# Layernorm folded into the first Fourier product of a GFNet + GEGLU block

## The chip, the cores and the metric

The kernel runs on one core of a Trainium2 chip. The metric is the device time of one execution in microseconds (us). TensorE is called PE in the profile, VectorE DVE, ScalarE ACT, GpSimd POOL; SP is the engine that issues most DMAs. PEld is TensorE's weight load.

## The reference

Two residual blocks are applied to x of 2048 rows by 576 columns, in bfloat16:

```python
def _layernorm(x, axis=-1, eps=1e-5):
    m = jnp.mean(x, axis=axis, keepdims=True)
    v = jnp.var(x, axis=axis, keepdims=True)
    return (x - m) / jnp.sqrt(v + eps)
...
    X = jnp.fft.rfft2(x.astype(jnp.float32), axes=(-2, -1))   # block A
    X = X * (w_r + 1j * w_i)
    y = jnp.fft.irfft2(X, s=(2048, 576), axes=(-2, -1)).astype(jnp.bfloat16)
...
    return (_gelu(x @ w_gate) * (x @ w_up)) @ w_down           # block B, 576 -> 4608 -> 576
...
    h = x + A(_layernorm(x));  h2 = h + B(_layernorm(h))
```

## The kernel before

The kernel has three parts. The **head** loads x, takes the layernorm statistics of its 16 tiles and does the first step of the row Fourier transform. The **spectral part** does the column transform, the rest of the row transform, the product with the filter and the way back. The **feed-forward part** is the gate and up products (L941), GELU, and the down product (L984, L1003), with the second layernorm spread among them. The change touches the head alone.

`h_sb` holds x as [128 partitions, 16 tiles h, 576]: row 16p + h lies on partition p of tile h. Six DMAs on SP's queue bring it in, for tiles 0-1, 2-3, 4-5, 6-7, 8-11 and 12-15 (L75). The 2048-row transform is split as 128 x 16, and `row16(h)` (L300) does the part over the 128 partitions of one tile: it multiplies the tile with the table `F16`, a 128 x 128 matrix of scaled sines that `row_table` builds (its zeros stand for the coset that a row does not belong to). Columns d and d + 288 are folded on the way: the product of the first half of the columns with [F, F] and of the second half with [F, -F] are added in PSUM, so 256 output columns hold sum and difference. So `F16` has three planes, F, F and -F, and `minus_row` makes the last. For each tile that is four products of 128 x 128 weights (a piece of the tile) with 256 moving columns (L308). The 64 + 64 remaining columns of each tile are done by `row16_rest` (L321), four tiles after another into one PSUM tile `f4`: two products of 64 weight columns with 128 moving columns for a tile (L324), in two column groups of the array.

The operand of these products is `xn`, a normalised copy of the tile: `norms(lo, hi)` (L362) has DVE write (x - mean) * rstd for one tile (L137), then calls `row16`. The statistics come in two ways. For tiles 0, 2, 4, 6, 8, 10 and 12 to 15 DVE does it (`sd`, L352: two bn_stats and, one tile later or by `flush`, a bn_aggr). For tiles 1, 3, 5, 7, 9 and 11 ACT does it (`ln_act`, L121: two passes with an accumulator, each followed by a read of the accumulator), and `ln_fin` on POOL turns the sum of squares into a variance. `ln_rstd` (L131) makes rstd for four tiles at a time on POOL, an addition and a power.

ACT takes the products out of PSUM into `Bt`: `evict` (L332) for two tiles at a time, `evict4` (L339) for the rests of four, the last of these on DVE. PSUM tiles with the tag "two" come from one ring of four; a new one waits until the one four before it has been read. `fill` (L295) issues products whose result nobody reads: 16 ahead of tile 0, 6 in `small_table`, 3 ahead of tile 8.

`small_table` (L401) transposes F by PE for the table `G16` of the way back. `phases`, `drop_sign`, `col_sin` and `mirror` make the column table `DT`: DVE computes phases `pd` and their absolute values `kd`, ACT takes the sines, and `mirror(r)` writes the second half as a signed mirror image, r = 1 on ACT and r = 0 on DVE. `first_a`, `angle_*`, `sine`, `cosine` and `minus_sine` make the table `TF` of the other part of the row transform. `gather(0)` and `gather(1)` (L370) are indirect DMAs of POOL's queue for the mirrored rows of the filter; SP's queue moves them into `WR` and `WI` later (L471), POOL scales two columns of these (L479), and DVE first uses them at L586.

The order of each engine's instructions is that of the program (`tc.manual_schedule()`), so the lines L414 to L490, written out by hand, are the schedule of the head. The first product of the spectral part is `f2` (L518), on `Bt`, `DT` and `DF`.

Of the kernel before, what the change touches and what calls it, by code (L numbers as in the profile page):

```python
# [42 lines left out]
def kernel_body(  # L43
# [44 lines left out]
    V.memset(mhalf[:], -0.5)  # L88

# [11 lines left out]
    F16 = keep.tile([P, 3, P], BF16, name="F16")  # L101
# [29 lines left out]
    def ln_rstd(dst, src, lo, hi):  # L131
        sl = slice(lo, hi)
        G.tensor_scalar(dst[:, sl], src[:, sl, 1], 1e-5, None, op0=ALU.add)  # L133
        G.tensor_tensor(dst[:, sl], dst[:, sl], mhalf[:, sl], ALU.pow)  # L134

# [137 lines left out]
    def phases():  # L273
        for t in range(3):
            V.scalar_tensor_tensor(
                pd[:, t, :], iJ[:], iD[:, t : t + 1], kd[:, t, :], op0=ALU.mult, op1=ALU.add
            )

    def row_table():
        V.scalar_tensor_tensor(  # L280
            F16[:, 0:2, :],
            iu[:].rearrange("p c l -> p (c l)").unsqueeze(1).to_broadcast([P, 2, P]),
            0.0,
            fs[:].unsqueeze(1).to_broadcast([P, 2, P]),
            op0=ALU.is_equal,
            op1=ALU.mult,
        )

    def minus_row():
        V.tensor_scalar(F16[:, 2, :], F16[:, 0, :], -1.0, None, op0=ALU.mult)  # L290

# [8 lines left out]
    def row16(h):  # L300
        if h % 2 == 0:
            ps_f[h] = two("f2t")
        f2t, b = (ps_f[h], 0) if h in ps_f else (ps_f[h - 1], 1)
        fill(f2t[:, b, :], FILL.get(h, 0))
        x = xn[:, h, :]
        for t in range(2):
            for n, d0 in ((0, t * P), (1, DH + t * P)):
                T.matmul(  # L308
                    f2t[:, b, t * 2 * P : (t + 1) * 2 * P],
                    lhsT=x[:, d0 : d0 + P],  # L310
                    rhs=F16[:, n : n + 2, :],
                    start=(n == 0),
                    stop=(n == 1),
                )

# [5 lines left out]
    def row16_rest(h):  # L321
        o = (h % 4) * P
        for p0, d0 in ((0, 256), (64, 512)):
            T.matmul(  # L324
                ps_f["f4", h - h % 4][p0 : p0 + 64, 0, o : o + P],
                lhsT=xn[:, h, d0 : d0 + 64],
                rhs=F16[:, 0, :],
                start=True,
                stop=True,
            )  # L330
# [16 lines left out]
    def flush():  # L347
        while agg:
            h, st = agg.pop()
            V.bn_aggr(mv[:, h, :], st[:])  # L350
# [11 lines left out]
    def norms(lo, hi):  # L362
        for h in range(lo, hi):
            normalise(V, xn[:, h, :], mv, rstd, h)
            row16(h)
# [11 lines left out]
    xn_pool = tc.tile_pool(name="xn", bufs=1, side="right")  # L377
    xn = xn_pool.__enter__().tile([P, H, D], BF16, name="xn")
# [10 lines left out]
    def mirror(r):  # L389

        for a in range(2):
            dst, src, sg = DT[:, :, a, r, JM - a : JH - a], DT[:, :, a, r, JM - 2 :: -1], sgn[:, r : r + 1]
            if r:
                A.activation(dst, src, ACT.Copy, scale=sg)
            else:
                V.tensor_scalar(dst, src, sg, None, op0=ALU.mult)
# [18 lines left out]
    for h in (1, 3, 5, 7, 9, 11):  # L415
        ln_act(h)
# [3 lines left out]
    sd(0, 2)  # L420
    minus_row()
    sd(4)
    ln_fin(slice(1, 4, 2))
    ln_rstd(rstd, mv, 0, 4)
    phases()
    sd(6)
    flush()
    norms(0, 4)
    rests(0)
    drop_sign(kd[:], pd[:])  # L430
    ln_fin(slice(5, 8, 2))
    ln_rstd(rstd, mv, 4, 8)
    gather(0)
    evict(0, 2)
    evict4(0)
    sd(8)
    norms(4, 8)
    rests(4)
    small_table()
    gather(1)  # L440
    sd(10, 12)
    ln_fin(slice(9, 12, 2))
    ln_rstd(rstd, mv, 8, 12)
    first_a()
# [5 lines left out]
    mirror(1)  # L450
    sd(13, 14, 15)
    flush()
    norms(8, 12)
    ln_rstd(rstd, mv, 12, 16)
    rests(8)
# [6 lines left out]
    evict4(8)  # L462
    mirror(0)
# [28 lines left out]
    xn_pool.__exit__(None, None, None)  # L492
# [570 lines left out]
```

## Time and profile before

| | |
|---|---|
| time, median of 3 runs | 495.87 us (495.71 to 495.88) |
| the profiled execution: its time, its span | 495.85 us, 494.1 us |
| instructions | 12754 |
| busy: PE, PEld, DVE, ACT, POOL | 484.4, 339.1, 223.8, 160.1, 28.9 us |
| granted TensorE clock | full in every slice |
| HBM | 111 GB/s over the span |

The span is the time between the first and the last instruction of the program that the profiler saw; the execution's own time has 1.75 us more around it. A row of the timeline has a start in us from the start of the span, the time the group took, engine, line, operation, tiles written and read, shape and count, and in brackets the engine's idle time before it with what ended it. PE's records overlap: a product's record holds its way through the array as well, so the distance from one start to the next is what it costs a stream.

### The profile page before, as it was taken

How to read it: one execution, taken by the hardware profiler on the slowest of the kernel's cores; microseconds unless marked ns; L12 is line 12 of the kernel's file. 1: busy time of each engine (PE TensorE's matmuls, PEld its weight loads, DVE VectorE, ACT ScalarE, POOL GpSimd, SP SyncE). 2: the span in 40 equal slices, each digit the busy share in tenths (PEclk: the TensorE clock that was granted, in tenths of full speed). 3: DMA queues.
4: the chain of work that ended last, by engine and by line, in shares of the span. 5: the costliest groups of instructions: out<-in, count | busy, mean ns of one | idle time of the engine just before them, and what ended most of it. 6: DMA issues, size and time to landing. Idle time of an engine off the chain costs nothing.

```text
span 494.1 us, 12754 instructions
## 1 busy us (share of the span) xinstructions
PE 484.4 (98%) x5711; PEld 339.1 (69%) x5711; DVE 223.8 (45%) x448; ACT 160.1 (32%) x285; POOL 28.9 (6%) x79
## 2 busy tenths in 40 slices
PE   6899999999999999999999999999999999999997
PEld 3578789875589955555599855555799655555995
DVE  8999784798622167433311344333121333333111
ACT  8999873333210022233200133232110232232000
POOL 8500010011110001000000000000000000000000
PEclk9999999999999999999999999999999999999999
DMA  8748978959990039987730079977700287770000
GB/s 282 211 91 154 253 137 219 181 107 217 209 194 3 1 101 179 211 159 146 146 71 3 19 173 187 195 148 146 145 3 1 85 159 154 156 146 3 13 15 24
DMA packets 89549, 62.33 MB, mean 126 GB/s; under 512 B 23190, under 2 KB 88086, under 8 KB 89494
## 3 DMA queue, kind: packets, MB, share of 16 engines
q1 hardware_dynamic: 89206, 60.34, 60.6%
q0 software_dynamic: 288, 1.18, 0.8%
q8 instruction: 44, 0.72, 0.7%
q14 instruction: 11, 0.09, 0.1%
HBM read 52.65 MB, written 2.36 MB: 111 GB/s over the span
## 4 chain that ended last, share of the span: by engine, by line
PE 93%; DVE 0%; issue 0%
PE gu L941 57%; PE acc L984 27%; PE cs_ps L677 2%; PE acc L1003 2%; PE eo_ps L626 2%; PE pq_ps L518 1%; PE y_ps L813 1%; PE gh_ps L536 1%; PE gh_ps L535 1%; PE eo_ps L650 0%; PE pt L882 0%; DVE h_sb L1010 0%
## 5 line engine op out<-in xcount | busy, mean ns | idle before, releaser
L941 PE MATMUL gu<-Bt,wgu 64*128 64x512 bf16 (+1 forms) x2646 | 270.7, 363 | 0.0
L941 PEld LDWEIGHTS <-wgu 64*128 64x128 bf16 x2646 | 152.5, 94 | 114.6 <-issue 0.3
L950 DVE TENSOR_TENSOR P_sb<-g_sb,gu 128x512 bf16<-128x512 f32 (+1 forms) x156 | 100.4, 645 | 140.3 <-ACT g_sb L949 140.3
L949 ACT ACTIVATE g_sb<-gu 128x512 f32<-128x512 f32 (+1 forms) x156 | 88.0, 564 | 193.5 <-PE gu L941 193.5
L984 PEld LDWEIGHTS <-P_sb 64*128 64x128 bf16 x2160 | 123.1, 94 | 9.9
L984 PE MATMUL acc<-wd,P_sb 64*128 64x288 bf16 x1440 | 90.9, 283 | 0.0
L993 DVE TENSOR_TENSOR part<-part,acc 128x576 f32<-128x576 f32 x15 | 11.3, 755 | 112.6 <-ACT part L992 112.6
L992 ACT COPY part<-acc 128x576 f32<-128x576 f32 x15 | 9.6, 639 | 122.8 <-PE acc L984 122.8
L984 PE MATMUL acc<-wd_a,P_sb 64*128 64x288 bf16 x720 | 46.8, 283 | 0.0
L518 PE MATMUL pq_ps<-DT,Bt 128*128 128x290 bf16 x64 | 12.3, 286 | 0.8 <-ACT Bt L334 0.8
L941 PE MATMUL gu<-Bt,wgu_e 64*128 64x256 bf16 (+1 forms) x162 | 12.5, 305 | 0.0
L838 DVE TENSOR_SCALAR hrow<-h_sb,mv,rstd 128x1152 bf16<-128x1152 bf16 x14 | 12.2, 869 | 0.6 <-POOL rstd L876 0.6
L995 DVE TENSOR_TENSOR h_sb<-h_sb,part 128x576 bf16<-128x576 bf16 x15 | 11.4, 758 | 0.5
L518 PEld LDWEIGHTS <-Bt 128*128 128x128 bf16 x96 | 9.2, 97 | 3.3 <-ACT Bt L334 1.0
L134 POOL TENSOR_TENSOR rstd<-rstd,mhalf 128x1 f32<-128x1 f32 (+1 forms) x16 | 11.2, 699 | 1.3
L941 PEld LDWEIGHTS <-wgu_e 64*128 64x128 bf16 x162 | 10.3, 94 | 1.2
L133 POOL TENSOR_SCALAR rstd<-mv 128x1 f32<-128x1 f32 (+1 forms) x16 | 4.2, 265 | 116.2 <-DVE mv L119 115.9
L677 PE MATMUL cs_ps<-DQ,EO 58*128 58x290 bf16 x144 | 10.8, 283 | 0.0
L298 PE MATMUL f2t<-h_sb,ident 128*128 128x512 bf16 x19 | 6.4, 503 | 3.9 <-DMA h_sb<-in_A_x_dram 3.7
L529 ACT CAST pq<-pq_ps 128x580 bf16<-128x580 f32 x15 | 9.8, 665 | 0.4 <-PE pq_ps L518 0.2
L677 PEld LDWEIGHTS <-EO 58*128 58x128 bf16 x160 | 7.8, 94 | 2.4 <-issue 0.7
L308 PE MATMUL f2t<-F,xn 128*128 128x256 bf16 x64 | 7.7, 273 | 1.3 <-DVE xn L137 1.3
(145 smaller groups left out, 278.9 us busy)
## 6 DMA issues: line engine op xcount, KB each, us to landing
wgu<-in_B_w_gate_dram SPq DMA_DIRECT2D x46, 432.0 KB, 5.2
wgu<-in_B_w_up_dram SPq DMA_DIRECT2D x46, 432.0 KB, 6.9
wd_a<-in_B_w_down_dram SPq DMA_DIRECT2D x1, 1728.0 KB
wd<-in_B_w_down_dram SPq DMA_DIRECT2D x1, 1728.0 KB
wd<-in_B_w_down_dram SPq DMA_DIRECT2D x6, 288.0 KB, 10.5
out_dram<-h_sb SPq DMA_DIRECT2D x3, 576.0 KB, 2.8
h_sb<-in_A_x_dram SPq DMA_DIRECT2D x4, 288.0 KB, 4.0
h_sb<-in_A_x_dram SPq DMA_DIRECT2D x2, 576.0 KB
```

The costliest lines, as they stand in the source:

```text
L134: G.tensor_tensor(dst[:, sl], dst[:, sl], mhalf[:, sl], ALU.pow)
L518: T.matmul(ps[:, par, 0:JP], lhsT=Bt[:, t, col], rhs=DT[:, t // 2, par] if t < 4 else DF[:, par], start=(t == par), stop=(t == 4),)
L626: T.matmul(pv[:, n], lhsT=z[:, a, w].rearrange("p b j -> p (b j)"), rhs=TI[:, ts[k], 1 - a : 3 - a, :], start=(a == 0), stop=(a == 1),)
L677: T.matmul(ps[:, e, 0:JP], lhsT=EO[x][rows, w, 2 * g : 2 * g + 2].rearrange("p h e k l -> p (h e k l)"), rhs=DQ[rows, w] if w or e else DT ...
L838: V.tensor_scalar(hrow[:], h_sb[:, h, :].rearrange("p (r k) -> p r k", k=64).unsqueeze(2).to_broadcast([P, NR, 2, 64]), mv2[:, h, 0:1], rs ...
L941: T.matmul(gu[:, c, 0:n], lhsT=w[rows, r, i * P : (i + 1) * P], rhs=hl[tcnk % 2][rows, r, lo:hi], start=(r == 0), stop=(r == NR - 1),)
L949: A.activation(g_sb, gu[:, 0, 0:n], ACT.Gelu_apprx_tanh)
L950: V.tensor_tensor(p_sb(f)[:, lo:hi], g_sb, gu[:, 1, 0:n], ALU.mult)
L984: T.matmul(accs[i][:, c, 0:DH], lhsT=p_sb(f)[rows, st * P : (st + 1) * P], rhs=wd[f // NWA][rows, f % NWA, c * DH : (c + 1) * DH], start=( ...
L993: V.tensor_tensor(part, part, accs[1][:, :, 0:DH], ALU.add)
L995: V.tensor_tensor(hv, hv, part, ALU.add)
L1003: T.matmul(acc[:, 0, 0:DH], lhsT=p_sb(f)[:, st * P : (st + 1) * P], rhs=wd[f // NWA][:, f % NWA, cc], start=(f == 0), stop=(f == NFT - 1),)
```

## The change

The copy `xn` goes. `row16` and `row16_rest` take the tile `h_sb` itself as weights, and the moving operand is a table for each tile, `FR[:, h]` = rstd * [F, -F], made by DVE: 256 columns where the copy had 576. `F16` loses its doubled plane; the [F, F] operand is one plane of `FR` read twice by a stride of zero.

What the subtraction of the mean did is done by a further product in PSUM: the weights are -2 * mean (for the sum half) or -mean (for the rests) of the tile's rows, read 128 or 64 times by a stride of zero from `mneg`, and the moving operand is rstd * F, 128 columns. That is two more products for a tile in `row16` and two more in `row16_rest`, 64 in all. `mneg` is made by POOL, `minus_means`, one instruction after each `ln_rstd`, from a constant `neg` that DVE sets at the start.

Tile 7's statistics move from ACT to DVE. `mirror(1)` moves from ACT to DVE and stands behind the last tiles' tables. Some instructions stand elsewhere: two of the three phases, `drop_sign`, `evict(0, 2)`, both gathers, the statistics of tiles 14 and 15 and the tables of tiles 8 to 11.

```diff
--- before.py
+++ after.py
@@ -86,6 +86,10 @@
     nhpib = const("nhpib", -0.5 * PI)
     mhalf = keep.tile([P, H], FP32, name="mhalf")
     V.memset(mhalf[:], -0.5)
+    neg = keep.tile([P, 2], FP32, name="neg")
+    for i in range(2):
+        V.memset(neg[:, i : i + 1], -2.0 + i)
+    mneg = keep.tile([P, 2, H], BF16, name="mneg")
 
 
 
@@ -98,7 +102,7 @@
     ]
     ident = keep.tile([P, P], BF16, name="ident")
 
-    F16 = keep.tile([P, 3, P], BF16, name="F16")
+    F16 = keep.tile([P, 2, P], BF16, name="F16")
     G16 = keep.tile([P, 2, 2, P], BF16, name="G16")
 
 
@@ -132,6 +136,15 @@
         sl = slice(lo, hi)
         G.tensor_scalar(dst[:, sl], src[:, sl, 1], 1e-5, None, op0=ALU.add)
         G.tensor_tensor(dst[:, sl], dst[:, sl], mhalf[:, sl], ALU.pow)
+
+    def minus_means(lo, hi):
+        sh = [P, 2, hi - lo]
+        G.tensor_tensor(
+            mneg[:, :, lo:hi],
+            mv[:, lo:hi, 0].unsqueeze(1).to_broadcast(sh),
+            neg[:].unsqueeze(2).to_broadcast(sh),
+            ALU.mult,
+        )
 
     def normalise(eng, dst, m, r, h):
         eng.tensor_scalar(
@@ -270,24 +283,24 @@
             TI[:, sl].rearrange("p k r q -> p (k r) q"), TF[:, sl].rearrange("p k r q -> p (k r q)"), transpose=True
         )
 
-    def phases():
-        for t in range(3):
+    def phases(*ts):
+        for t in ts:
             V.scalar_tensor_tensor(
                 pd[:, t, :], iJ[:], iD[:, t : t + 1], kd[:, t, :], op0=ALU.mult, op1=ALU.add
             )
 
     def row_table():
         V.scalar_tensor_tensor(
-            F16[:, 0:2, :],
-            iu[:].rearrange("p c l -> p (c l)").unsqueeze(1).to_broadcast([P, 2, P]),
+            F16[:, 0, :],
+            iu[:].rearrange("p c l -> p (c l)"),
             0.0,
-            fs[:].unsqueeze(1).to_broadcast([P, 2, P]),
+            fs[:],
             op0=ALU.is_equal,
             op1=ALU.mult,
         )
 
     def minus_row():
-        V.tensor_scalar(F16[:, 2, :], F16[:, 0, :], -1.0, None, op0=ALU.mult)
+        V.tensor_scalar(F16[:, 1, :], F16[:, 0, :], -1.0, None, op0=ALU.mult)
 
     ps_f = {}
     FILL = {0: 16, 8: 3}
@@ -302,16 +315,24 @@
             ps_f[h] = two("f2t")
         f2t, b = (ps_f[h], 0) if h in ps_f else (ps_f[h - 1], 1)
         fill(f2t[:, b, :], FILL.get(h, 0))
-        x = xn[:, h, :]
+        x = h_sb[:, h, :]
+        plus = FR[:, h, 0:1, :].to_broadcast([P, 2, P])
         for t in range(2):
             for n, d0 in ((0, t * P), (1, DH + t * P)):
                 T.matmul(
                     f2t[:, b, t * 2 * P : (t + 1) * 2 * P],
                     lhsT=x[:, d0 : d0 + P],
-                    rhs=F16[:, n : n + 2, :],
+                    rhs=FR[:, h] if n else plus,
                     start=(n == 0),
-                    stop=(n == 1),
+                    stop=False,
                 )
+            T.matmul(
+                f2t[:, b, t * 2 * P : t * 2 * P + P],
+                lhsT=mneg[:, 0, h : h + 1].to_broadcast([P, P]),
+                rhs=FR[:, h, 0, :],
+                start=False,
+                stop=True,
+            )
 
     def rests(h):
         ps_f["f4", h] = two("f4")
@@ -320,14 +341,15 @@
 
     def row16_rest(h):
         o = (h % 4) * P
-        for p0, d0 in ((0, 256), (64, 512)):
-            T.matmul(
-                ps_f["f4", h - h % 4][p0 : p0 + 64, 0, o : o + P],
-                lhsT=xn[:, h, d0 : d0 + 64],
-                rhs=F16[:, 0, :],
-                start=True,
-                stop=True,
-            )
+        for mean in (False, True):
+            for p0, d0 in ((0, 256), (64, 512)):
+                T.matmul(
+                    ps_f["f4", h - h % 4][p0 : p0 + 64, 0, o : o + P],
+                    lhsT=mneg[:, 1, h : h + 1].to_broadcast([P, 64]) if mean else h_sb[:, h, d0 : d0 + 64],
+                    rhs=FR[:, h, 0, :],
+                    start=not mean,
+                    stop=mean,
+                )
 
     def evict(*hs):
         for h in hs:
@@ -361,7 +383,7 @@
 
     def norms(lo, hi):
         for h in range(lo, hi):
-            normalise(V, xn[:, h, :], mv, rstd, h)
+            V.tensor_scalar(FR[:, h], F16[:], rstd[:, h : h + 1], None, op0=ALU.mult)
             row16(h)
 
     wm = [tmp(n, [P, 8 * J], BF16) for n in ("wm_r", "wm_i")]
@@ -374,8 +396,8 @@
             in_offset=bass.IndirectOffsetOnAxis(ap=rev[:, 0:1], axis=0),
         )
 
-    xn_pool = tc.tile_pool(name="xn", bufs=1, side="right")
-    xn = xn_pool.__enter__().tile([P, H, D], BF16, name="xn")
+    fr_pool = tc.tile_pool(name="FR", bufs=1, side="right")
+    FR = fr_pool.__enter__().tile([P, H, 2, P], BF16, name="FR")
 
     def col_sin(r, src, bias):
         A.activation(
@@ -390,10 +412,7 @@
 
         for a in range(2):
             dst, src, sg = DT[:, :, a, r, JM - a : JH - a], DT[:, :, a, r, JM - 2 :: -1], sgn[:, r : r + 1]
-            if r:
-                A.activation(dst, src, ACT.Copy, scale=sg)
-            else:
-                V.tensor_scalar(dst, src, sg, None, op0=ALU.mult)
+            V.tensor_scalar(dst, src, sg, None, op0=ALU.mult)
 
     G16v = [G16[:, sign].rearrange("p x q -> p (x q)") for sign in range(2)]
     pt = []
@@ -412,47 +431,52 @@
                 )
 
     first, rest = slice(0, 2), slice(2, 9)
-    for h in (1, 3, 5, 7, 9, 11):
+    for h in (1, 3, 5, 9, 11):
         ln_act(h)
     G.memset(DF[:], 0.0)
     G.memset(DT[:, :, 1, :, JH - 1], 0.0)
     row_table()
-    sd(0, 2)
+    sd(0)
     minus_row()
-    sd(4)
+    sd(2, 4)
     ln_fin(slice(1, 4, 2))
     ln_rstd(rstd, mv, 0, 4)
-    phases()
-    sd(6)
+    minus_means(0, 4)
+    phases(0)
+    sd(6, 7)
     flush()
+    ln_fin(slice(5, 6))
+    ln_rstd(rstd, mv, 4, 8)
+    minus_means(4, 8)
+    gather(0)
     norms(0, 4)
     rests(0)
-    drop_sign(kd[:], pd[:])
-    ln_fin(slice(5, 8, 2))
-    ln_rstd(rstd, mv, 4, 8)
-    gather(0)
-    evict(0, 2)
-    evict4(0)
     sd(8)
     norms(4, 8)
     rests(4)
+    phases(1, 2)
     small_table()
-    gather(1)
+    evict(0, 2)
+    evict4(0)
     sd(10, 12)
+    drop_sign(kd[:], pd[:])
     ln_fin(slice(9, 12, 2))
     ln_rstd(rstd, mv, 8, 12)
+    minus_means(8, 12)
+    gather(1)
     first_a()
     col_sin(1, pd, zerob)
     col_sin(0, kd, hpib)
     evict(4, 6)
     evict4(4)
     A.activation(G16v[0], pt[0][:, 0, 0 : 2 * P], ACT.Copy, scale=G_SCALE)
-    mirror(1)
-    sd(13, 14, 15)
+    sd(13)
+    norms(8, 12)
+    rests(8)
+    sd(14, 15)
     flush()
-    norms(8, 12)
     ln_rstd(rstd, mv, 12, 16)
-    rests(8)
+    minus_means(12, 16)
     angle_b(first)
     angle_s(first)
     angle_c(first)
@@ -460,6 +484,7 @@
     rests(12)
     evict(8, 10)
     evict4(8)
+    mirror(1)
     mirror(0)
     V.tensor_copy(DF[0:32], D3[0:32])
     V.tensor_copy(DF[96:128], D3[96:128])
@@ -489,7 +514,7 @@
 
     load_dq(1)
 
-    xn_pool.__exit__(None, None, None)
+    fr_pool.__exit__(None, None, None)
     spw = tc.tile_pool(name="spw", bufs=1)
     wk = spw.__enter__()
     m1, m2 = (wk.tile([P, 2, 2, JP], BF16, name=n) for n in ("m1", "m2"))
```

## The prediction

> **What bounds the kernel now.** I read the page's chain first, then the chain of waits in order of time for the first 75 us, then the timeline of each engine through the head.
>
> ```profile
> span 494.1 us, 12754 instructions
> 31.09 0.04 issue
> 31.13 0.28 PE gh_ps L536
> ```
>
> The last two lines are the first pieces of the chain in order of time: from 31.13 us on it is TensorE without a break, to the end. So what the head does to the time is what it does to PE's start at 31.13, one for one. Next, PE's timeline up to there.
>
> ```profile
> 3.66 5.58 PE L298 MATMUL f2t<-h_sb,ident 128*128 128x512 bf16 x16 [3.66 <-DMA h_sb<-in_A_x_dram]
> 9.07 1.91 PE L308 MATMUL f2t<-F,xn 128*128 128x256 bf16 x16
> 10.91 0.41 PE L324 MATMUL f<-F,xn 128*64 128x128 bf16 x8
> 11.90 1.92 PE L308 MATMUL f2t<-F,xn 128*128 128x256 bf16 x16 [0.58 <-DVE xn L137]
> 13.76 0.41 PE L324 MATMUL f<-F,xn 128*64 128x128 bf16 x8
> 14.10 1.47 PE L298 MATMUL pt<-h_sb,ident 128*128 128x512 bf16 x6
> 15.50 0.30 PE L406 MATMUL pt<-ident,F 128*64 128x128 bf16 x4
> 16.08 0.81 PE L298 MATMUL f2t<-h_sb,ident 128*128 128x512 bf16 x3 [0.28 <-ACT Bt L334]
> 17.43 1.92 PE L308 MATMUL f2t<-F,xn 128*128 128x256 bf16 x16 [0.54 <-DVE xn L137]
> 19.28 0.41 PE L324 MATMUL f<-F,xn 128*64 128x128 bf16 x8
> 19.91 1.92 PE L308 MATMUL f2t<-F,xn 128*128 128x256 bf16 x16 [0.21 <-DVE xn L137]
> 22.97 0.67 PE L518 MATMUL pq_ps<-DT,Bt 128*128 128x290 bf16 x4 [0.80 <-ACT Bt L334]
> 30.60 0.30 PE L535 MATMUL gh_ps<-pq,TF 128*128 128x289 bf16 x1 [0.27 <-ACT TF L263]
> 31.13 0.28 PE L536 MATMUL gh_ps<-pq,TF 128*128 128x289 bf16 x1 [0.23 <-ACT pq L529]
> ```
>
> The four L308 rows are the four groups of tiles, each with its rests (L324). PE waits ahead of groups two, three and four: it is not the bound of the head. Who is, ACT's and DVE's rows show:
>
> ```profile
> 10.98 0.67 ACT L124 ACTIVATE junk<-h_sb 128x576 bf16<-128x576 bf16 x1
> 11.64 1.90 ACT L334 CAST Bt<-f2t 128x1024 bf16<-128x1024 f32 x2
> 17.58 0.85 ACT L394 ACTIVATE DT<-DT,sgn 128x216 bf16<-128x216 bf16 x2
> 20.99 1.93 ACT L334 CAST Bt<-f2t 128x1024 bf16<-128x1024 f32 x2
> 24.95 1.04 ACT L260 ACTIVATE TF<-pr,pib 128x896 bf16<-128x896 int32 x1 [0.38 <-DVE pr L251]
> 7.29 0.45 DVE L357 BATCH_NORM_STATS2 st<-h_sb 128x6 f32<-128x288 bf16 x1
> 8.20 0.21 DVE L350 BATCH_NORM_AGGREGATE mv<-st 128x2 f32<-128x12 f32 x1
> 8.42 1.45 DVE L137 TENSOR_SCALAR xn<-h_sb,mv,rstd 128x576 bf16<-128x576 bf16 x4
> 22.21 0.69 DVE L340 CAST Bt<-f 128x512 bf16<-128x512 f32 x1 [0.16 <-PE f L324]
> 24.00 0.26 DVE L266 TENSOR_SCALAR TF<-TF 128x256 bf16<-128x256 bf16 x1
> ```
>
> ACT's statistics last until 11.64, its first eviction begins there, and the last pair (20.99 + 1.93 = 22.92) releases the spectral part's first product at 22.97. The last tile's products are read at once: the fourth of these groups ends PE's work for ACT at about 21.86 (19.91 + 1.92 and the signal), and ACT's last eviction starts near 21.90. So the head ends with three engines nearly level, and PE's share of it is the start at 9.07, its work, and its waits.
>
> **The change part by part: what leaves.** ACT loses one pair of statistics passes, 2 x (11.64 - 10.98) = 1.33 us, and the two mirrors, 0.85. DVE's copy of a tile, 1.45 / 4 with the overlap, some 0.34 us from start to start, becomes a table of 256 columns. The nearest row is L266 with the same shape, 0.26 as a record and less than 0.2 from start to start: about 0.15 saved on each of 16 tiles, 2.4 us. DVE gains the statistics of tile 7, 0.8 us (from the start at 7.29 to the aggregate at 8.20, less the last step's latency), and mirrors which on DVE take about the 0.27 each that r = 0 does now. POOL gains four small `minus_means`. All of this would matter if ACT and DVE still set the end; next is why I think they don't.
>
> **What PE gains.** I need the price of three forms.
>
> ```profile
> L308 PEld LDWEIGHTS <-xn x64: 95/98/99, 8.9 to 21.4; 128*128 128x128 bf16 x64
> L308 PE MATMUL f2t<-F,xn x64: 272/273/283, 9.1 to 21.6; 128*128 128x256 bf16 x64
> L324 PE MATMUL f<-F,xn x32: 219/219/243, 10.9 to 21.9; 128*64 128x128 bf16 x32
> 56.24 1.31 PE L650 MATMUL eo_ps<-TI,Zt 128*64 128x128 bf16 x40
> ```
>
> A 256-column product costs the stream (1.91 - 0.27) / 15 = 0.109 us; those four for a tile stay. In the rests, two products run side by side in two column groups: by the L650 row a pair costs (1.31 - 0.22) / 19 = 0.057. The rests of a group go from 4 pairs to 8, so 0.23 more for a group.
>
> The mean's product in `row16` is in no row: 128 x 128 weights with only 128 moving columns. Call its step s. Low end: the pair above has the same number of weight columns and of moving columns in 0.057. High end: after it, the next tile piece must be in the array, and a full-width load's record is 0.098; no full-width load in the head follows another by less than 0.109. The two rows are equally near (one has the moving side, the other the weights), so I take the middle, s = 0.077, and keep 0.057 to 0.109 for the range. The Trainium skill ("TensorE: Matmul & The Clock Gate", Back-to-back issue gap) gives about 81 ns for a sustained stream of a load and a 128-column product; with that step the sum below is 0.12 us higher. Nothing in this trace has that form.
>
> Working time of a group now: 14.10 - 11.90 = 2.20 us, with no wait inside. So PE's waits are 11.90 - (9.07 + 2.20) = 0.63; the table stage ends at about 15.74 (two pairs and the way back to full width after 15.50), so 16.08 - 15.74 = 0.34; three fills of (1.47 - 0.38) / 5 = 0.216 end at 16.73, so 17.43 - 16.73 = 0.70; and 19.91 - (17.43 + 2.20) = 0.28. Together 1.95 us. (The brackets print less, since a record's tail covers some of it.)
>
> Can PE start before 9.07? No: its 16 fills run from 3.66 without a break (0.35 each, against 0.216 later on) and end there. The first table needs rstd, as the copy did, and DVE's statistics of tile 7 before it: of the three phases two leave, 2 x 0.28, and 0.8 come, so it starts at 8.42 + 0.25, or later if tiles 6 and 7 land after 6.7. With 0.26 for the table that is 8.9 to 9.2; I take 0.08 late.
>
> ```profile
> 5.64 0.46 DVE L357 BATCH_NORM_STATS2 st<-h_sb 128x6 f32<-128x288 bf16 x1 [0.25 <-DMA h_sb<-in_A_x_dram]
> 6.45 0.92 DVE L275 SCALAR_TENSOR_TENSOR pd<-iJ,iD,kd 128x146 f32<-128x146 f32 x3
> 5.64:8.50 2.86, 2.86 (x10) 1.13 (x9) 2.82 (x11) 2.86 (x11) 2.50 (x9) 1.00 0.99 364
> ```
>
>  After that no wait is left in sight: rstd for tiles 4 to 7 comes a little sooner, since one square sum is waited for instead of two, and PE comes to them 0.7 us later; the tables of tiles 8 to 11 no longer stand behind the statistics of tiles 14 and 15, two times 0.8; those of 12 to 15 stand behind as much DVE work as their copies did or less, so they come by 19.9, and PE by the sum below comes to them at 20.5. So the added work fills the waits first and then pushes.
>
> Sum up to the last tile's last product, which releases ACT's last eviction: 31 steps s before it, three rests of 0.23, one more full step of 0.109 in front of it and 0.054 less for its shorter record (0.219 against 0.273): 2.39 + 0.69 + 0.055 = 3.13. Less the waits, 1.95, less the 0.04 by which ACT came after PE, plus 0.08: **+1.2 us** for the spectral part's start. For s = 0.057 it is +0.6, for 0.098 +1.9, for 0.109 +2.2.
>
> DVE's `evict4` at 22.21 waits for the last rests, which gain 32 s + 0.92: +1.5 us. DVE runs without a gap from it to the first spectral tile, and ACT's sine at 24.95 waits for DVE's row L251, so this second delay travels too.
>
> ```profile
> 31.79 0.46 DVE L607 TENSOR_TENSOR Zt<-zb,za 128x580 bf16<-128x580 bf16 x1
> 32.73 1.25 PE L626 MATMUL eo_ps<-TI,Zt 128*128 128x256 bf16 x10
> 9.66 0.59 POOL L133 TENSOR_SCALAR rstd<-mv 128x4 f32<-128x4 f32 x1
> 13.30 0.95 POOL L370 DMA_INDIRECT wm_i<-in_A_w_i_dram,rev  x1 [0.30 <-issue]
> 23.96 0.43 POOL L479 TENSOR_SCALAR WI<-WI 128x34 bf16<-128x34 bf16 x1 [2.73 <-DMA WI<-wm_i]
> 29.27 0.76 DVE L586 TENSOR_TENSOR m<-xab,WI 128x1156 bf16<-128x1156 bf16 x1
> ```
>
> PE uses DVE's first tile 32.73 - 32.25 = 0.48 us after it is done. So 1.5 - 0.45 is still under PE's own 1.2, and the latter decides. PE's two waits for ACT at 30.60 and 31.13 don't absorb it: the ACT chain in front of them hangs on the late sine and the late products.
>
> **What costs nothing.** `minus_means` is a POOL operation on eight columns; one on four took 0.59 at its slowest (beside DVE's copies). Begun at about 8.5, when rstd is there, it is done by 9.1, and the third product of tile 0 wants it near 9.35; later groups have their margin. The second gather now waits behind rstd for tiles 8 to 11 and starts about 2 us later than 13.30; its data is ready at 24.40 and DVE wants it at 29.27, so 2.9 us of cover remain, and SP's queue behind it waits for DVE's tables anyway. ACT's saving is smaller than 1.33 + 0.85: a tile's two passes sooner, it reaches tile 9 at 11.64 - 3 x 1.33 = 7.65, and tiles 8 to 11 aren't there yet. Tiles 4 and 5 came at 5.64 (the row above), and the six tiles of the next two loads, 128 x 576 bf16 or 147 KB each, take 2.4 us at the 364 GB/s of that window (its last column) even if nothing else moved: 8.1 at the earliest, an estimated 8.5 with the filter's load beside them. All of this lies under PE's delay. The sum is on the execution of 495.85 us, 0.02 under the median: 495.85 + 1.2 = 497.05.
>
> **The rivals.**
>
> *No change that can be told.* A measurement of this kernel can tell about 0.2%, 1.0 us, from no change. If the load hides behind the short product, s = 0.057 and the delay is 0.6: 496.45. For it: a load of 0.098 is hidden behind each 0.109 stream of the L308 rows. Against: no row hides one behind a stream half as long. It decides from s = 0.070 down. The Trainium skill (same page, "Wait — 56ns, not 53.3ns?") has 55 to 56 ns between 128-column products; by that rule this rival wins, and no run here shows it at full width.
>
> *Faster, since ACT sets the end.* If PE kept up, ACT would begin its evictions at 8.5 + 2 x 1.33 = 11.2 us and not at 11.64, and run without the mirrors: 0.4 + 0.85 + some 0.1 of small waits = 1.4 us sooner, 494.45. Price and place are good, but it needs PE's extra 3.1 us to shrink under some 0.6, so the mean's products would have to run beside the others at almost no cost. The only rows with products side by side use different column groups.
>
> *Worse, a load of stride zero or at full price.* If each full-width load takes the 0.109 that I never see undercut, +2.2: 498.05. For: that spacing bounds every full-width row. Against: 0.109 is also just 256 columns' streaming, and the 290-column rows take longer, so the stream may be all it shows.
>
> *The filter's gather late* by more than its 2.9 us of cover would add to DVE's start instead; I see nothing that does that.
>
> **How the numbers follow.** PE as the new bound with s between 0.070 and 0.109 and so a delay over 1.0 us: 0.52, and the forecast is its middle, 497.0. The same mechanism with the load hidden: 0.37. Faster through ACT, or something in the later schedule that I don't see: 0.11. The range runs from 496.2 (s = 0.057 and no late start, +0.35 to +0.5) to 498.1 (s = 0.109), and leaves out the faster case and the tails.
>
> **What would show it.** Right: from 9.1 us PE has no wait of over 0.1 us in the head, the groups last about 3.0 us (2.20 + 8 x 0.077 + 0.23), the first L518 row starts near 24.2, and ACT waits for PE ahead of the evictions of tiles 8 to 15. Wrong: a step after the mean's product near 0.057, so groups of 2.9 and a start near 23.6; or PE still waiting for DVE's tables; or the spectral part's chain taking back part of the delay, which I priced at nothing.

## The result and the profile after

| | before | after |
|---|---|---|
| time, median of 6 runs each | 495.88 us (495.71 to 496.28) | 498.40 us (498.33 to 498.54) |
| ratio, 95% interval | | 1.005 (1.0038 to 1.0063) |
| the profiled execution: its time, its span | 495.85 us, 494.1 us | 498.44 us, 496.7 us |

The kernel became slower by 2.5 us. The forecast was +1.2 us, with a range that ends at 498.1 us: the sign was right, the size was not. The spans differ by 2.6 us, and two places of the profile after hold all of it. Lines have moved: the four products of a tile are L322 (before: L308), the mean's product is L329, the rests L346 (L324), the evictions L356 and L362, the tables L386, the first spectral product L543 (L518), the gate and up products L966 (L941).

From the page of the changed kernel, the span and the group of the gate and up products. The last column is idle time of PE ahead of this group:

```profile
span 496.7 us, 12884 instructions
...
L966 PE MATMUL gu<-Bt,wgu 64*128 64x512 bf16 (+1 forms) x2646 | 270.6, 363 | 1.3 <-issue 1.3
```

From its chain of work in order of time (start, duration, what):

```profile
32.24 0.28 PE gh_ps L561
...
67.88 2.40 PE gu L966 x44
70.28 1.30 issue
71.58 25.24 PE gu L966 x424
```

The unbroken work of TensorE begins at 32.24 us and not at 31.13: +1.11, which is what the forecast was about. But it isn't unbroken. At 70 us, 46 us behind the code that was changed, PE stops, and "issue" means that it waited for nothing that the profile shows. PE's timeline there, the kernel before first and then the changed one:

```profile
69.12 4.09 PE L941 MATMUL gu<-Bt,wgu 64*128 64x256 bf16 x72
```

```profile
69.03 1.25 PE L966 MATMUL gu<-Bt,wgu 64*128 64x256 bf16 x18
71.58 1.60 PE L966 MATMUL gu<-Bt,wgu 64*128 64x256 bf16 x26 [1.30 <-issue]
```

The last product ahead of the gap starts at 70.01, the next at 71.58; a step in this stream is 0.054, so 1.5 us are lost. 1.11 + 1.5 = 2.6: the whole difference of the spans.

PE's timeline through the head after the change:

```profile
9.62 0.38 PE L322 MATMUL f2t<-FR,h_sb 128*128 128x256 bf16 x2
9.84 0.22 PE L329 MATMUL f2t<-FR,mneg 128*128 128x128 bf16 x1
9.90 0.38 PE L322 MATMUL f2t<-FR,h_sb 128*128 128x256 bf16 x2
...
12.48 0.39 PE L322 MATMUL f2t<-FR,h_sb 128*128 128x256 bf16 x2
...
15.35 1.47 PE L311 MATMUL pt<-h_sb,ident 128*128 128x512 bf16 x5
...
17.64 0.38 PE L322 MATMUL f2t<-FR,h_sb 128*128 128x256 bf16 x2
...
20.50 0.39 PE L322 MATMUL f2t<-FR,h_sb 128*128 128x256 bf16 x2
...
23.97 0.67 PE L543 MATMUL pq_ps<-DT,Bt 128*128 128x290 bf16 x4 [0.54 <-ACT Bt L356]
```

No row between 9.62 and 23.2 has a bracket: all four waits of PE are gone. The mean's product takes 9.90 - 9.84 = 0.056 us until the next product starts, and a group 12.48 - 9.62 = 2.86. The first spectral product starts at 23.97 instead of 22.97, +1.00. On the other engines, ACT and then DVE:

```profile
8.59 0.68 ACT L128 ACTIVATE junk<-h_sb 128x576 bf16<-128x576 bf16 x1 [0.77 <-DMA h_sb<-in_A_x_dram]
...
11.27 1.90 ACT L356 CAST Bt<-f2t 128x1024 bf16<-128x1024 f32 x2
...
18.94 2.11 ACT L356 CAST Bt<-f2t 128x1024 bf16<-128x1024 f32 x2 [1.46 <-PE f2t L329]
...
21.80 2.11 ACT L356 CAST Bt<-f2t 128x1024 bf16<-128x1024 f32 x2 [0.27 <-PE f2t L329]
```

```profile
8.94 0.82 DVE L386 TENSOR_SCALAR FR<-F,rstd 128x256 bf16<-128x256 bf16 x4
...
19.42 1.09 DVE L386 TENSOR_SCALAR FR<-F,rstd 128x256 bf16<-128x256 bf16 x4 [0.68 <-POOL rstd L138]
...
23.47 0.69 DVE L362 CAST Bt<-f 128x512 bf16<-128x512 f32 x1 [1.51 <-PE f L346]
```

ACT and DVE now wait for PE (1.46, 0.27, 1.51): the work that was taken from them came back as waiting time, and PE is the bound of the head.

Why did PE begin at 9.62 and not at 9.07? Its 16 fills end there. The windows of one microsecond show when they went over to the shorter spacing (PE's busy time, and behind it in parentheses the number of its instructions; the granted clock reads 1.00 throughout). Before, then after:

```profile
7.00:8.00 1.00, 1.00 (x5) 0.41 (x4) 1.00 (x5) 1.00 (x4) 0.92 (x2) 1.00 1.02 369
8.00:9.00 1.00, 1.00 (x6) 0.48 (x5) 0.96 (x4) 1.00 (x5) 0.58 (x2) 1.00 0.99 372
```

```profile
7.00:8.00 1.00, 1.00 (x4) 0.33 (x3) 0.91 (x4) 0.82 (x4) 0.92 (x2) 1.00 0.94 341
8.00:9.00 1.00, 1.00 (x5) 0.38 (x4) 0.97 (x5) 0.41 (x1) 0.84 (x4) 1.00 1.00 382
```

The spacing fell about 1 us later in the execution after. In the ten kernels here with the same 16 fills, one profiled execution each, the last fill's record ends between 8.88 and 10.02 us where the head begins as before, and between 8.80 and 9.79 where it begins as changed. So the 0.55 us does not follow the change from kernel to kernel. That it differs as much between executions of one kernel is not shown: the six times of the changed kernel lie within 0.21 us, though PE has no wait left there that could take up a late start. The Trainium skill ("TensorE: Matmul & The Clock Gate", What's actually happening) says that the array's clock rises at the end of a window that runs freely, so that the moment of the rise varies by half a microsecond either way. The spread here, 1.2 us from the first to the last end, is of about that size; no run here shows the window itself.

### The profile page after: what moved, and what is told of

It reads as the page before. It is cut to its first block, busy times and chain, and to the rows that moved or that the text cites. A ratio compares the mean times of both kernels' runs of the same rounds, so it can differ in the third digit from the quotient of the medians.

```text
span 496.7 us, 12884 instructions
## 1 busy us (share of the span) xinstructions
PE 487.4 (98%) x5774; PEld 336.2 (68%) x5775; DVE 222.7 (45%) x455; ACT 158.4 (32%) x279; POOL 29.2 (6%) x83
## 4 chain that ended last, share of the span: by engine, by line
PE 93%; issue 0%; DVE 0%
PE gu L966 56%; PE acc L1009 27%; PE cs_ps L702 2%; PE acc L1028 2%; PE eo_ps L651 2%; PE pq_ps L543 1%; PE y_ps L838 1%; PE gh_ps L561 1%; PE gh_ps L560 1%; PE eo_ps L675 0%; PE pt L907 0%; DVE h_sb L1035 0%
## 5 line engine op out<-in xcount | busy, mean ns | idle before, releaser
L966 PE MATMUL gu<-Bt,wgu 64*128 64x512 bf16 (+1 forms) x2646 | 270.6, 363 | 1.3 <-issue 1.3
L966 PEld LDWEIGHTS <-wgu 64*128 64x128 bf16 x2646 | 148.8, 94 | 119.6 <-issue 1.8
L543 PE MATMUL pq_ps<-DT,Bt 128*128 128x290 bf16 x64 | 12.3, 286 | 0.5 <-ACT Bt L356 0.5
L966 PE MATMUL gu<-Bt,wgu_e 64*128 64x256 bf16 (+1 forms) x162 | 12.3, 305 | 0.0
L543 PEld LDWEIGHTS <-Bt 128*128 128x128 bf16 x96 | 9.2, 97 | 3.1 <-ACT Bt L356 0.7
L138 POOL TENSOR_TENSOR rstd<-rstd,mhalf 128x1 f32<-128x1 f32 (+1 forms) x16 | 11.2, 700 | 1.3
L966 PEld LDWEIGHTS <-wgu_e 64*128 64x128 bf16 x162 | 9.0, 94 | 2.4
L322 PE MATMUL f2t<-FR,h_sb 128*128 128x256 bf16 x64 | 9.2, 273 | 0.0
```

The source lines that it names most:

```text
L543: T.matmul(ps[:, par, 0:JP], lhsT=Bt[:, t, col], rhs=DT[:, t // 2, par] if t < 4 else DF[:, par], start=(t == par), stop=(t == 4),)
L966: T.matmul(gu[:, c, 0:n], lhsT=w[rows, r, i * P : (i + 1) * P], rhs=hl[tcnk % 2][rows, r, lo:hi], start=(r == 0), stop=(r == NR - 1),)
```

## The experiments

The theory for the gap: TensorE's instructions themselves are fetched by DMA, and the changed kernel ran out of them. The page of the kernel before counts 5711 matmuls and 5711 weight loads on TensorE and 44 packets on the instruction queue q8; the page after 5774, 5775 and 45. That is some 257 to 260 instructions of TensorE to a packet. The 64 added products and their 64 loads are 128 instructions, half a packet, so that every later boundary between packets falls on other work. Counted in the trace, with 10 instructions of its sequencer beside 730 products and 732 weight loads, the gap lies behind TensorE's 1472nd instruction. Where the queues' packets stand, from the DMA part of the changed kernel's page (queue, kind: packets, MB, the packets' times added up as a share of 16 engines' time), for 63 to 68.7 us and for 68.7 to 70.2 us:

```profile
q1 hardware_dynamic: 1533, 1.15, 112.4%
```

```profile
q1 hardware_dynamic: 49, 0.03, 12.2%
q8 instruction: 1, 0.02, 5.7%
```

Until 68.7 the four early loads of gate and up weights (`wgu_e`, issued from 58.81 on) fill the DMA engines, and no instruction packet moves. It starts at 68.79 as these loads run out, takes 1.37 us, and PE goes on 1.42 us behind its end. The rival: the gap has to do with something else that the change moved (buffers, semaphores, the data of the loads), or the head's delay grows on its way.

**The products alone.** The kernel before with 64 added products whose weights are zeros, so that they add nothing; all else is as before.

```diff
+            T.matmul(f2t[:, b, t * 2 * P : t * 2 * P + P], lhsT=mzero[:, 0:1].to_broadcast([P, P]),
+                     rhs=F16[:, 0, :], start=False, stop=True)
...
-        for p0, d0 in ((0, 256), (64, 512)):
+        for mean in (False, True):
+            for p0, d0 in ((0, 256), (64, 512)):
...
+                    lhsT=mzero[:, 0:1].to_broadcast([P, 64]) if mean else xn[:, h, d0 : d0 + 64],
```

> The kernel before, with its normalised copy and its order, plus the 64 further products of the change, here with weights that are zero. Theory W (TensorE's extra products alone make the loss: they first fill its waits of about 1.95 us in the head and then push, 0.5 us at steps of 0.056; and the 128 further instructions move the place where TensorE runs out of fetched ones, which costs about 1.5 us near 70 us): first spectral product near 23.5, a break of 1 to 2 us with no wait shown among the first gate products, 497.4 to 498.4. Rival S (the loss comes from the moved statistics, mirrors and gathers, the products fit the waits): no break, 495.9.

Measured: 497.93 us (497.86 to 498.16), ratio 1.0042 (1.0026 to 1.0059). Its chain's first row, and PE's timeline at the gap:

```profile
32.05 0.28 PE gh_ps L546
```

```profile
68.73 1.37 PE L951 MATMUL gu<-Bt,wgu 64*128 64x256 bf16 x22
71.07 2.14 PE L951 MATMUL gu<-Bt,wgu 64*128 64x256 bf16 x36 [0.97 <-issue]
```

Four fifths of the loss, 2.0 of 2.5 us, come from these products alone, the late chain (32.05) and the gap (69.83 to 71.07, behind the 1473rd instruction by the same count) among them. What was moved to DVE and what ACT was spared are not in this kernel.

**As many instructions without the work.** The kernel before with the 16 + 6 fills cut into four products each: 66 more products, but no more columns.

```diff
+        w = 512 // cut
...
+            for i in range(cut):
+                T.matmul(dst[:, i * w : (i + 1) * w], lhsT=ident[:],
+                         rhs=h_sb[:, 0, i * w : (i + 1) * w], start=True, stop=True)
```

> The kernel before, with the fills ahead of tile 0 and of the small table cut into four pieces of 128 columns: the same streaming, 66 more products and as many loads, nothing else. Theory F (the break near 70 us depends on how many instructions TensorE has behind it when the weights' transfers keep its instruction fetch waiting): a break of 1 to 3 us among the first gate products, 497 to 499, while the head stays as it was, first spectral product near 23.0. Rival D (the break comes because the changed head is 1 us later against the transfers): no break, 495.9.

Measured: 496.43 us (495.85 to 496.96), ratio 1.0011 (1.0002 to 1.0021): neither theory's time. The ten executions fall into two groups, five at 495.85 to 496.21 and five at 496.65 to 496.96. The one that was profiled (496.00) belongs to the faster group and has no gap; whether the slower ones have one is not on record. So the count does not make the gap in every execution, and more than that isn't shown. In the profiled one the packet started at 65.45, beside the loads, and PE came to the end of its 1472nd instruction at 68.93, some 0.65 us after the packet was usable (65.45 + 1.41 + 1.42 = 68.28, with the 1.42 of the changed kernel). Why the packet moved 3.3 us sooner, when PE was only 1.1 us further ahead (68.93 against 70.01), is not settled.

The same execution shows what PE's waits in the head are worth. PE's first row of tile products and its first spectral products:

```profile
9.92 1.91 PE L311 MATMUL f2t<-F,xn 128*128 128x256 bf16 x16
...
23.11 0.67 PE L521 MATMUL pq_ps<-DT,Bt 128*128 128x290 bf16 x4 [0.80 <-ACT Bt L337]
```

The former starts 0.85 us later than in the kernel before, the latter only 0.14 later: the waits took up the rest.

**The changed kernel without its mean products.** It leaves out the subtraction of the mean; tables, statistics and order are those after.

```diff
-            T.matmul(f2t[...], lhsT=mneg[:, 0, h : h + 1].to_broadcast([P, P]), ...)
...
-        for mean in (False, True):
+        for mean in (False,):
```

> The changed kernel without the 64 products of the mean: the subtraction of the mean is left out, all else is as changed. Theory W and F: no break near 70 us, since TensorE has as many instructions as before; the head's end then waits for rstd of tiles 12 to 15 and the first spectral product starts near 22.7; 495.4 to 495.9. Rival S: the moved work costs time without the products too, so 496.5 or more.

Measured: 496.38 us (495.92 to 496.88), ratio 1.0011 (1.0002 to 1.0021), and no gap in the profiled execution (496.13, one of the faster of ten). The time lies between the two forecasts. So without the price the change still gains nothing. PE's timeline says why:

```profile
20.21 1.91 PE L322 MATMUL f2t<-FR,h_sb 128*128 128x256 bf16 x16 [1.59 <-DVE FR L379]
```

The tables of tiles 12 to 15 come when POOL has rstd, which waits for the statistics of tiles 14 and 15; with less work on PE this wait stands bare. Everything that DVE was spared by the smaller tables sits ahead of a wait.

**The changed kernel without fills.** The 6 fills of `small_table` and the 3 ahead of tile 8 go, 1.9 us of PE's work.

```diff
-    FILL = {0: 16, 8: 3}
+    FILL = {0: 16}
...
-        fill(pt[0][:, 1, :], 6)
+        fill(pt[0][:, 1, :], 0)
```

> The changed kernel without the 6 fills in the small table and the 3 ahead of tile 8, nothing else. Theory W: TensorE is the bound of the head, so 1.9 us of its work less lets the first spectral product start near 23.0 and not 23.97, where rstd of tiles 12 to 15 takes over as the bound; 497.4 if the break near 70 us stays, 496.0 if 18 instructions fewer and 1 us earlier take it away. Rival: TensorE's clock drops without the fills and gains are lost: 498.4 or more.

Measured: 498.18 us (497.55 to 498.53), ratio 1.0042 (1.0025 to 1.0059). PE's timeline:

```profile
10.02 0.38 PE L322 MATMUL f2t<-FR,h_sb 128*128 128x256 bf16 x2 [1.16 <-DVE FR L386]
...
16.69 0.38 PE L322 MATMUL f2t<-FR,h_sb 128*128 128x256 bf16 x2 [0.77 <-DVE FR L386]
...
20.99 0.38 PE L322 MATMUL f2t<-FR,h_sb 128*128 128x256 bf16 x2 [1.38 <-DVE FR L386]
...
24.45 0.67 PE L543 MATMUL pq_ps<-DT,Bt 128*128 128x290 bf16 x4 [0.54 <-ACT Bt L356]
```

Neither of the first theory's times came: PE's freed time turned into waits for DVE's tables. In this execution, the slowest of four, DVE could begin with tile 6 only at 7.90, against 7.09 in the changed kernel, and with tile 7's statistics on DVE the first table stands behind that. A lower clock is not the reason: the way from the last group's start to the first spectral product takes 24.45 - 20.99 = 3.46 us, in the changed kernel 23.97 - 20.50 = 3.47. PE's fills covered DVE; they were not what held the head up. The gap is there too (70.93 to 72.13).

**The gap removed.** The changed kernel, but the second of the two early gate and up loads is issued later, behind `flip(3)`. The number of TensorE's instructions stays.

```diff
-    pre += [load_gu(3 + i, early[:, i]) for i in range(2)]
+    pre += [load_gu(3, early[:, 0]), early[:, 1]]
...
-        2: [(norm2, 3), (flip, 3), (load_wd, 1)],
+        2: [(norm2, 3), (flip, 3), (load_late, 4), (load_wd, 1)],
```

> The changed kernel with the second of the two early gate/up loads (864 KB) issued later, behind the transposed row 3 and ahead of the down weights, and not back to back with the first; its first use is over 10 us after that. Theory F2 (TensorE's instruction fetch, asked for near 63 us, waits behind these loads until they end near 68.8 us and so comes too late for the 128 instructions more): the fetch starts before 66 us, no break near 70 us, 497.0, which is the head's delay of about 1.1 us alone. Rival D (the break comes from the later head as such): break stays, 498.4.

Measured: 497.34 us (497.14 to 497.76), ratio 1.0032 (1.002 to 1.0045). The DMA part for 65 to 66.5 us, and PE's timeline where the gap was:

```profile
q8 instruction: 1, 0.02, 4.9%
q1 hardware_dynamic: 5, 0.00, 0.9%
```

```profile
68.64 4.62 PE L969 MATMUL gu<-Bt,wgu 64*128 64x256 bf16 x80
```

With half of the loads gone from that stretch the instruction packet moves at 65.09, 3.7 us sooner, and PE runs through. This separates the theories: neither the products nor the buffers changed, only the time of one pair of loads and with it the DMA traffic ahead of the packet. The time is 0.3 us above the forecast of 497.0, since the head of the profiled execution was later again (its chain starts at 32.51 instead of 32.24). The two controls of this edit follow: in the kernel before, which has no gap to lose, and in the kernel before with zero products, which has one.

> The kernel before with the same later load, as a control. Theory F2: there was no break to remove, so 495.9 within 0.2. Rival (the later load helps or hurts the feed-forward part by itself): 495.4 or less, or 496.4 or more.

> The kernel before with the 64 zero products, and with the later load. Theory W with F2: the break near 70 us goes, the head's delay of about 0.9 us stays: 496.8 within 0.2, against 497.93 with the load where it was. Rival D: the break stays, 497.9.

Measured: 495.92 us (495.68 to 496.18) for the first, ratio 1.0001 (0.9992 to 1.0011), so the later load by itself does nothing; 496.97 us (496.72 to 497.27) for the second, ratio 1.0021 (1.0012 to 1.003), against 497.93 with the gap. The second's timeline and the first row of its chain:

```profile
68.72 4.53 PE L954 MATMUL gu<-Bt,wgu 64*128 64x256 bf16 x80
```

```profile
32.48 0.28 PE gh_ps L546
```

So the gap is worth 497.93 - 496.97 = 0.96 us here and 498.40 - 497.34 = 1.06 in the changed kernel by the medians, 1.2 to 1.5 by the profiles with it. The medians give less because the heads of the kernels without the gap were later (32.51 against 32.24, 32.48 against 32.05). What stays, 1.1 to 1.5 us by the medians, is the head's delay.

**Tile 7 back on ACT.** Late load as above; tile 7's statistics are ACT's again.

```diff
-    for h in (1, 3, 5, 9, 11):
+    for h in (1, 3, 5, 7, 9, 11):
...
-    sd(6, 7)
+    sd(6)
```

> The later load as in the run before, and of the change tile 7's statistics are put back on ACT. Theory W (TensorE's work from the end of the fills is the bound of the head): 497.0 within 0.3, ACT's first eviction near 12.2 instead of 11.3 with no effect; the first table no longer hangs on the load of tiles 6 and 7. Rival (the statistics on DVE delay the first table and that is the loss): 496.5 or less.

Measured: 497.14 us (496.94 to 497.37), ratio 1.0027 (1.0017 to 1.0037). PE's first product came at 8.83, 0.98 sooner than in the kernel with the late load alone (9.81, of which 0.21 was a wait for the table and the rest the fills' later end), but the first spectral product at 23.95, only 0.29 sooner:

```profile
20.49 0.38 PE L322 MATMUL f2t<-FR,h_sb 128*128 128x256 bf16 x2 [0.73 <-DVE FR L386]
```

An earlier start is again spent ahead of the last four tables.

**Three other orders of the head**, all with the late load, to see whether the change can be made to pay. The first takes tile 7's statistics behind the first tables and drops the 9 later fills; the second has tile 7 on ACT, 13 fills ahead of tile 0 and none later, all statistics and rstd ahead of the last two phases, the sines and the mirrors, and the third eviction of rests on DVE; the third puts that eviction back on ACT, `angle_a(rest)` behind the last tables and `mirror(1)` ahead of the first angles.

```diff
-    FILL = {0: 16, 8: 3}
+    FILL = {0: 13}          # second and third; first: {0: 16}
...
+    sd(8, 10)
+    flush()
+    ln_fin(slice(9, 12, 2))
+    ln_rstd(rstd, mv, 8, 12)
...
+    sd(12, 13, 14)
     norms(8, 12)
     rests(8)
+    sd(15)
     flush()
     ln_rstd(rstd, mv, 12, 16)
...
     norms(12, 16)
     rests(12)
+    angle_a(rest)           # third alone, these three lines
+    evict4(8)
+    mirror(1)
```

> A version that might beat both: the changed kernel with the later load, without the 6 and the 3 fills, with the tables of tiles 0 to 3 ahead of tile 7's statistics, the sums of tiles 8 to 12 taken earlier, and ACT's sines behind the second pair of evictions. Theory W with F2: TensorE's work is 1.9 us less, so with the tables in time the first spectral product starts near 22.1 to 22.4 against 22.97 before, and there is no break: 495.0 to 495.4. Rival (DVE and POOL can't have the tables ready in time): 495.9 or more, with waits for the tables of tiles 8 or 12.

> A second try for a version that beats both: the changed kernel with the later load, tile 7's statistics on ACT, 13 fills ahead of tile 0 and none later, statistics of tiles 10 and 12 to 15 taken earlier, both gathers ahead of the rstd that they stood behind, ACT's sines behind the second pair of evictions, and the third rests' eviction on DVE. Theory W: TensorE has 2.6 us of work less and the tables come before it wants them (tiles 8 near 15.4, tiles 12 near 18), so the first spectral product starts near 21.9 against 22.97: 494.6 to 495.2. Rival (the tables or the filter's rows come late): 495.7 or more, with waits for the tables or for the filter ahead of its first product.

> As the kernel of the run before (late second gate/up load, tile 7 on ScalarE, 13 fills), with ScalarE's sine for the rest of the angles ahead of the tables' mirrors and of the fourth eviction of the third group, the third group's rests evicted on ScalarE again, and the first mirror earlier. If the 0.68 us that TensorE waited at 23.2 for VectorE's eviction was only a matter of order, the first spectral product is near 22.4, no wait over 0.3 follows it before 26, the spectral chain starts near 30.6 (before: 31.13), and the time is 495.3 to 495.6. Rival: the head of the kernel holds as much work on VectorE and ScalarE as on TensorE, so that another wait takes the place of the one removed; then the chain starts at 31.1 to 31.4 and the time is 495.9 to 496.3.

Measured: first, 497.34 us (497.13 to 497.81), ratio 1.003 (1.0019 to 1.0042); second, 496.10 us (495.82 to 496.34), ratio 1.0003 (0.9994 to 1.0012); third, 495.60 us (495.51 to 495.83), ratio 0.9994 (0.9985 to 1.0003). PE's timelines of the first and of the second:

```profile
20.83 0.38 PE L322 MATMUL f2t<-FR,h_sb 128*128 128x256 bf16 x2 [1.77 <-DVE FR L386]
```

```profile
21.88 0.67 PE L544 MATMUL pq_ps<-DT,Bt 128*128 128x290 bf16 x4 [0.31 <-ACT Bt L356]
23.22 0.42 PE L544 MATMUL pq_ps<-DF,Bt 128*128 128x290 bf16 x2 [0.68 <-DVE Bt L362]
```

The first and the second came out as their rivals had it. The first waits for the tables of tiles 12 to 15. The second reached the first spectral product 1.1 us sooner than before, then stood for DVE's eviction of the third rests. The third removed that wait and got another. Its rows on PE, ACT and DVE:

```profile
22.73 0.67 PE L544 MATMUL pq_ps<-DT,Bt 128*128 128x290 bf16 x4 [1.10 <-DVE DF L492]
```

```profile
20.72 1.95 ACT L356 CAST Bt<-f2t 128x1024 bf16<-128x1024 f32 x2
```

```profile
22.36 0.31 DVE L492 COPY DF<-DT 32x580 bf16<-32x580 bf16 x1
```

ACT's last pair ends at 20.72 + 1.95 = 22.67, DVE's copy at 22.36 + 0.31 = 22.67, and PE, done with its rests at about 21.6, waits for both. The chain then starts at 31.11 us, as before at 31.13. The best order of the changed computation that I found can't be told from the kernel before: all three engines are level at the end of the head. That is the expectation's rival for the chain, while the time came in at the top of the first theory's range.

## Why the prediction missed

**The bound of the head: right.** PE's 1.95 us of waits went, PE ran without a wait from its first table on, and ACT and DVE wait for it. The head's delay travelled on undiminished: +1.00 at the first spectral product, +1.11 at the start of the chain. The forecast was +1.2.

**But the +1.2 was made of a wrong step and a missing one.** The mean's product was put at 0.077, between bounds of 0.057 and 0.109; it takes 0.056, the lower bound, and a group 2.86 us instead of 3.0. By the prediction's own sum that is +0.6, the rival of no change. The load of full width did hide behind a product half as long. The Trainium skill ("TensorE: Matmul & The Clock Gate", Wait — 56ns, not 53.3ns?) gives this number, and the trace agrees (0.056); the 81 ns of its Back-to-back issue gap, which I weighed as well, show nowhere in these runs for this form. What made up for the mis-sized step, by luck, was the start: 9.07 was taken as fixed by the fills, with 0.08 for a late table. The table was in time, but the fills ended later and the start was 9.62, +0.55, in this execution. Why the fills end later in one profiled execution than in another is open. What a late start costs is shown: with the waits of the kernel before, 0.85 us of it became 0.14 (the kernel with cut fills); with the waits filled, the later head of the kernel with the late load, 9.81 against 9.62, was paid in full, 24.24 against 23.97, and in the two kernels with zero products 0.42 of 0.61 us was paid (starts at 9.25 and 9.86, first spectral products at 23.78 and 24.20). That the change takes away this protection was not in the sum.

**The step that failed** is the sentence that TensorE runs without a break from 31.13 us to the end, so that the head's effect is felt one for one. That held for the delay, but it put nothing for the count of instructions, and PE lost 1.5 us at a break near 70 us. The DMA part of the kernel before for 67.7 to 70.2 us shows the packet in question:

```profile
q8 instruction: 1, 0.02, 3.4%
```

This packet, which PE needs behind its 1472nd instruction, starts at 67.78 and takes 1.38; with the 1.42 us that PE took after the packet's end later, it is usable at about 70.6, and PE comes there at 72.40: a margin of 1.8 us that no view of the page names. The change draws on it twice. The 128 more instructions bring that point forward by 64 steps of 0.054, 3.5 us, less the 1.1 of delay: 2.4. The head's delay brings the loads, and with them the packet, 1.0 later (68.79). 1.8 - 2.4 - 1.0 = -1.6; the gap measures 1.5. This sum was made afterwards, and the kernel with cut fills does not follow it in its profiled execution, since its packet came early. The late load, in two kernels, shows that the break goes when the packet comes sooner. The prediction had only "something in the later schedule that I don't see", in one chance with the faster case.

**The side terms.** ACT waited for tiles 8 to 11 (first read at 8.59; estimated 8.5) and began its evictions at 11.27 (11.2): right. The last tables came at 19.42 ahead of PE's 20.50, as said, though by a margin that the experiments used up at once. The filter's cover held: POOL had scaled `WI` at 26.9, and DVE used it at 30.52. Nothing of the delay was taken back in the spectral part. Of the rivals, "faster, since ACT sets the end" is refuted by the kernel without mean products, which has PE's work of before and is not faster: then DVE's and POOL's last tables set the end.

## What to carry to other kernels

When an edit adds instructions to one engine, count them as a load on its instruction fetch as well: find the engine's instruction queue on the page, divide its instructions by its packets, and look where a boundary falls beside heavy data transfers; an idle time put down to "issue", far from the edit, is the sign. Waits in the critical engine are not only loss: they absorb a late start, and a change that fills them can make a late start count in full. Where three engines are level at the end of a stage, taking work from two of them buys waiting time, and the order has to be rebuilt for all three before the trade can even break even.

## What the hardware showed that was not expected

- TensorE's instructions come in packets of 16 KB (0.74 MB in 45 packets), one to some 257 of its instructions. The packet in question took 1.12 to 1.52 us in the thirteen kernels, and PE went on 1.3 to 1.4 us behind its end in the three kernels with a gap (71.58 - 70.16, 71.07 - 69.80, 72.13 - 70.82).
- Behind a stretch of data loads the packet starts as they run out: 68.79, 68.55 and 69.51 us in the kernels with a gap, 64.23 to 65.09 in the three with half of the loads moved away and as many products. The exception is the kernel with cut fills (65.45 with all loads in place, in an execution of its faster group), which no run here explains. In the changed kernel without the later fills the profile names the load's end as what ended the gap, though the products behind it read other weights; an inferred releaser can be a neighbour of the true one.
- A product of 128 columns with weights of full width, read by a stride of zero, costs 0.056 us; a weight load of 0.097 to 0.098 hid behind each.
